# Reciprocals on a folded 96x6 tile, one key-sum addition open to two engines, weights converted by alternate eights, and PSUM banks dealt anew after batch 0

## Chip, cores and metric

The kernel runs on one core of one Trainium2 chip. The metric is the device time of one execution in microseconds (us). Five instruction streams matter: TensorE (PE in the profile, with its weight loads as PEld), VectorE (DVE), ScalarE (ACT), GpSimd (POOL) and SyncE (SP), which issues all the DMAs.

## What is computed

An attention over pooled queries feeds a two-layer network without a bias. Cut to what matters:

```python
q_pool = q.reshape(B, H, S // 2, 2, D).mean(axis=3)       # B, H, S, D = 4, 8, 1152, 64
scores = q_pool @ k^T / sqrt(D);  scores -= max(scores)    # 576 x 1152 for each head
attn   = exp(scores) / (sum(exp(scores)) + 1e-9)
x      = (attn @ v) of all heads side by side              # 2304 x 512
h      = x @ w_in;  g = maximum(0.01 * h, h);  out = g @ w_out   # d_ff = 2048
```

All inputs are float32 except for the weights, which arrive as float64 and are converted on the chip.

## The kernel before

**Stages.** There are 32 heads (4 batches of 8). For each head `k_tr`, `q_sum` and `q_tr` bring keys and queries into transposed form, each split in a high and a low part; `qk` (15 matmuls) with `vmax` (a DVE maximum of each result) and `vneg` find the row maxima, which `m_cp` and `m_dma` write into the query tile. A head has two units `u` of 288 queries. For each unit five groups `qkt` (four matmuls, the last group two) write scores into a PSUM slot `s`, `exp` on ACT empties the slot into one of seven tiles `e`, `esum` adds the five tiles up in five additions (four of them over the tiles, the last folding the two halves), and `pv` multiplies with the values. `norm` collects the two halves of `pv`. When both units are done, `r_mm` (L424) sums over the keys' partitions, `r_cp` (ACT) copies the sums to the tile `rs`, `r_inv` (L442) takes their reciprocals on all 128 x 288 elements, `scale` (POOL) multiplies and `x_out` writes the head's part of x to DRAM.

The second part works on 9 blocks of 256 rows of x. `l1` (L552: 16 chunks `f` of w_in with 12 matmuls of 256 columns each) fills PSUM tiles `ml`, `post` (ACT, then DVE or ACT, then POOL) makes the high and low parts `gg`, and `l2` (L574 to L576: three matmuls of 512 columns for each `f`) accumulates eight `f` in another `ml` tile, twice for each half of the rows. Block 0 needs batch 0 of x, so no `l1` can run before head 7's `x_out`.

**Weights.** Each of the 16 chunks of w_in and of w_out goes through `w_load` (DMA), `w_f32` in five steps (L484 ACT, L489 and L493 DVE, L497 ACT, L500 POOL), `w_hi` (a cast on DVE or ACT) and `w_lo` (L509 POOL); for w_in `w_out_dma` writes the result to DRAM, and `ws_load` fetches it for every block. All 16 chunks of w_in are converted first, then the 16 of w_out.

**What sets the order.** A planner in the kernel (`Scheduler`) takes steps by priority and by its own costs and writes one fixed instruction order for each engine. A step names the engines that may do it, and the planner takes the one that would be done first. PSUM has eight banks, dealt by name: `s` has two slots of two banks (0 and 1, 2 and 3), `t` (transposes, `qk`, `r_mm`) banks 4 and 7, with bank 6 until batch 0 is done, `o` (`pv`) bank 5, and `ml` bank 6 from then on; behind the last `pv` `ml` has six more.

```python
tags["s"] = [(None, 0, slots("bank", (0, 1), (2, 3)))]
tags["ml"] = [(early, 0, slots("bank", (6,))), (tail, 0, slots("bank", (0,), (1,), (2,), (3,), (4,), (7,)))]
step(esum, u, NX, prio=pu - 3, eng={"POOL": gp(HW)}, deps=[("esum", u, NX - 1)])
step(r_inv, hd, prio=pu - 2, eng={"DVE": 0.15 + 8 * HW / 960.0}, deps=... [("r_cp", hd)])
```

Of the kernel before, what the change touches and what calls it, by code (L numbers as in the profile page):

```python
# [149 lines left out]
def tile_pooled_attention_moe(  # L150
# [246 lines left out]
    def by_pe(hd):  # L397
        return hd < PESUM

    def over_keys(p, u, w):  # L400
        for x in range(NX):
            ts = kts(x)
            for a in range(2):
                if len(ts) == 2:
                    t, c = ts[a], slice(0, HW)
                    s = ex[u, x][:, a]
# [7 lines left out]
    def pv(u, e, i, i2=None):
        po[u] = new("o", i)
        over_keys(po[u], u, lambda t: vv[u // 2][:, t, :])
        if i2 is not None:
            rps[u] = new("t", i2)
            over_keys(rps[u], u, lambda t: ones)
# [361 lines left out]
```

## Time and profile before

| what | us |
|---|---|
| median of 3 runs | 1021.51 |
| the runs | 1017.75 to 1022.74 |
| the profiled execution | 1023.68 |
| its span, first to last instruction | 1021.9 |
| PE busy in the span | 934.3 |
| POOL, DVE, ACT busy | 634.0, 568.3, 426.4 |
| mean granted TensorE clock | 0.968 of full |

A busy time is a sum over the instructions of an engine, waits for a shared port inside an instruction among it. The granted clock is the share of full speed that TensorE was given: 1.0 is 2.4 GHz and 0.5 is 1.2 GHz. Heads are told apart in the trace by `r_mm`, which stands once in each.

### The profile page before, as it was taken

How to read it: one execution, taken by the hardware profiler on the slowest of the kernel's cores; microseconds unless marked ns; L12 is line 12 of the kernel's file. 1: busy time of each engine (PE TensorE's matmuls, PEld its weight loads, DVE VectorE, ACT ScalarE, POOL GpSimd, SP SyncE). 2: the span in 40 equal slices, each digit the busy share in tenths (PEclk: the TensorE clock that was granted, in tenths of full speed). 3: DMA queues.
4: the chain of work that ended last, by engine and by line, in shares of the span. 5: the costliest groups of instructions: out<-in, count | busy, mean ns of one | idle time of the engine just before them, and what ended most of it. 6: DMA issues, size and time to landing. Idle time of an engine off the chain costs nothing.

```text
span 1021.9 us, 16164 instructions
## 1 busy us (share of the span) xinstructions
PE 934.3 (91%) x5920; PEld 741.2 (73%) x5920; DVE 568.3 (56%) x934; ACT 426.4 (42%) x856; POOL 634.0 (62%) x548
## 2 busy tenths in 40 slices
PE   6888886978978898999999999999999999999998
PEld 2665654647845687777777778787788898989896
DVE  5799888787778888766666666666211111010100
ACT  3565654545655556555445545544221111111110
POOL 3688888578978889867657767748832222232320
PEclk9998988989978999999999999999999999999999
DMA  9264444365514236435415345214386565666640
GB/s 262 88 200 156 151 128 126 106 214 187 208 58 151 85 116 191 133 86 163 135 53 173 110 122 174 85 51 141 95 260 211 195 207 184 201 207 208 212 154 31
DMA packets 96943, 153.72 MB, mean 150 GB/s; under 512 B 9408, under 2 KB 63840, under 8 KB 96864
## 3 DMA queue, kind: packets, MB, share of 16 engines
q1 hardware_dynamic: 96864, 152.68, 47.8%
q8 instruction: 47, 0.77, 0.3%
q14 instruction: 32, 0.26, 0.1%
HBM read 125.30 MB, written 17.83 MB: 140 GB/s over the span
## 4 chain that ended last, share of the span: by engine, by line
PE 71%; DVE 10%; issue 5%; ACT 5%; POOL 4%; DMA 3%; SPq 2%; DVEq 0%; ACTq 0%; POOLq 0%
PE banks L552 19%; PE banks L410 12%; PE banks L347 9%; PE banks L378 6%; PE banks L379 6%; PE banks L574 5%; PE banks L575 5%; PE banks L576 5%; DVE stat L351 3%; DMA xb<-xd 2%; SPq L530 2%; DVE raw L493 1%; PE banks L424 1%; DVE raw L489 1%; ACT qh L325 1%
## 5 line engine op out<-in xcount | busy, mean ns | idle before, releaser
L351 DVE TENSOR_REDUCE stat<-banks 128x1 f32<-128x384 f32 (+1 forms) x480 | 255.0, 550 | 106.5 <-PE banks L347 94.2
L552 PE MATMUL banks<-xb,ws 128*128 128x256 f32 x1728 | 238.5, 285 | 9.4 <-issue 3.1
L552 PEld LDWEIGHTS banks<-xb,ws 128*128 128x128 f32 x1728 | 225.6, 191 | 20.4 <-issue 5.7
L384 ACT ACTIVATE e<-banks 128x576 f32<-128x576 f32 (+1 forms) x320 | 183.9, 600 | 128.8 <-PE banks L379 62.6
L392 POOL TENSOR_TENSOR sm<-sm,e 128x576 f32<-128x576 f32 (+1 forms) x192 | 234.9, 1242 | 0.5
L347 PE MATMUL banks<-ka,qh 128*128 128x384 f32 (+1 forms) x480 | 176.7, 399 | 38.2 <-DVE ql L329 20.0
L378 PE MATMUL banks<-qh,ka 128*128 128x288 f32 x576 | 172.9, 316 | 12.9 <-ACT e L384 12.0
L379 PE MATMUL banks<-ql,kb 128*128 128x288 f32 x576 | 165.1, 302 | 0.3 <-DMA ql<-ms 0.3
L410 PE MATMUL banks<-e,vv 128*64 128x288 f32 (+1 forms) x1280 | 164.5, 406 | 0.4 <-ACT e L384 0.4
L347 PEld LDWEIGHTS banks<-ka,qh 128*128 128x128 f32 (+1 forms) x480 | 86.8, 190 | 77.3 <-DVE stat L351 30.3
L410 PEld LDWEIGHTS banks<-e,vv 128*64 128x64 f32 x1280 | 90.3, 144 | 71.9 <-issue 23.0
L565 POOL TENSOR_TENSOR gg<-g,gg 128x512 fp32r<-128x512 f32 x50 | 64.9, 1298 | 116.3 <-DVE gg L191 106.6
L378 PEld LDWEIGHTS banks<-qh,ka 128*128 128x128 f32 x576 | 112.4, 195 | 28.5 <-ACT e L384 23.1
L560 ACT ACTIVATE g<-banks 128x512 f32<-128x512 f32 x72 | 43.1, 598 | 214.2 <-PE banks L552 214.0
L392 POOL TENSOR_TENSOR sm<-e 128x576 f32<-128x576 f32 x64 | 91.8, 1451 | 58.5 <-PE banks L424 53.2
L379 PEld LDWEIGHTS banks<-ql,kb 128*128 128x128 f32 x576 | 112.5, 195 | 1.3 <-DMA ql<-ms 0.5
L574 PE MATMUL banks<-wo,gg 128*128 128x512 f32 x200 | 81.1, 406 | 0.6 <-ACT raw L191 0.3
L191 DVE CAST gg<-g 128x512 fp32r<-128x512 f32 x40 | 21.8, 546 | 106.0 <-ACT g L560 106.0
L565 POOL TENSOR_TENSOR ka<-g,ka 128x512 fp32r<-128x512 f32 x22 | 28.3, 1288 | 81.3 <-DVE ka L191 70.7
L575 PE MATMUL banks<-wo,gg 128*128 128x512 f32 x200 | 78.5, 393 | 0.0
L576 PE MATMUL banks<-wo,gg 128*128 128x512 f32 x200 | 78.3, 392 | 0.0
L442 DVE RECIPROCAL rs<-rs 128x288 f32<-128x288 f32 x32 | 62.4, 1949 | 12.3 <-ACT rs L428 12.0
(61 smaller groups left out, 1066.4 us busy)
## 6 DMA issues: line engine op xcount, KB each, us to landing
ws<-wd SPq DMA_DIRECT2D x144, 512.0 KB
kn<-in_k_dram SPq DMA_DIRECT2D x32, 288.0 KB
qn<-in_q_dram SPq DMA_DIRECT2D x32, 288.0 KB
vv<-in_v_dram SPq DMA_DIRECT2D x32, 288.0 KB
raw<-in_moe_w_in_dram SPq DMA_DIRECT2D x16, 512.0 KB
kb<-ka SPq DMA_DIRECT2D x64, 128.0 KB
wd<-ws SPq DMA_DIRECT2D x16, 512.0 KB
raw<-in_moe_w_out_dram SPq DMA_DIRECT2D x16, 512.0 KB
```

The source lines that it names most:

```text
L347: nc.tensor.matmul(p, lhsT=qh[hd][:, o:o + n], rhs=ka[hd][:, c * CW:(c + 1) * CW], start=True, stop=True)
L351: nc.vector.tensor_reduce(out=mx[hd][:n, i, c:c + 1], in_=mps.pop((hd, i, c)), axis=AX.X, op=ALU.max)
L378: nc.tensor.matmul(p[:, a, :HW], lhsT=ka[hd][:, ks], rhs=qh[hd][:, c], start=True, stop=False)
L379: nc.tensor.matmul(p[:, a, :HW], lhsT=kb[hd][:, ks], rhs=ql[hd][:, c], start=False, stop=True)
L384: nc.scalar.activation(out=ex[u, x][:, :n], in_=sps.pop((u, x))[:, :n, :HW], func=AF.Exp)
L392: ENG[e].tensor_tensor(out=a, in0=ex[u, 0][:, :n] if x == 1 else a, in1=ex[u, x][:, :n], op=ALU.add)
L410: nc.tensor.matmul(p[64 * a:64 * a + 64, c], lhsT=w(t), rhs=s, start=(x == 0), stop=(x == NX - 1))
L552: nc.tensor.matmul(p, lhsT=wst[i, f][:, a, c, :], rhs=xx[i][:, x, c, :], start=(n == 0), stop=(n == 3 * KC - 1))
L565: ENG[e].tensor_tensor(out=t[:, 1], in0=gf.pop((i, fp)), in1=f32(t[:, 0]), op=ALU.subtract)
L574: nc.tensor.matmul(p, lhsT=gh, rhs=wo[f][:, 0], start=(f == hf * FH), stop=False)
L575: nc.tensor.matmul(p, lhsT=gh, rhs=wo[f][:, 1], start=False, stop=False)
L576: nc.tensor.matmul(p, lhsT=gl, rhs=wo[f][:, 0], start=False, stop=(f == hf * FH + FH - 1))
```

## The change

- **Reciprocals.** `r_cp` is followed by `r_fold` (two small DMAs that fold one row of each half of `rs` into a tile `rt` of 96 x 6), `r_inv` on `rt`, `r_row` (a DMA of `rt` to DRAM) and `r_wide` (two DMAs that spread it over the 128 partitions of `rs` again). `rs` has two buffers in place of one.
- **Key sums.** The addition `x == 2` of each unit may go to DVE, at the planner's cost plus 0.4; the fixed order puts 54 of the 64 there.
- **Weights.** The order is eight chunks of w_in, eight of w_out, eight of w_in, eight of w_out; `w_hi` is on ACT alone; `w_load` may run four ahead instead of three, and the priorities change.
- **PSUM.** When batch 0 is done, `s` keeps one slot (0 and 1), `t` gets bank 2 and `ml` bank 3 beside bank 6.
- The branch `by_pe`, which `PESUM = 0` had switched off, is gone.

```diff
-PESUM = 0
+DX = (2,)
+CONT = 0.4
-WAHEAD = 3
-WIN = (30.0, 0.5)
+WAHEAD = 4
+WIN = (40.0, 0.5)
...
-        "rs": (1, [128, HW], F32, sb),
+        "rs": (2, [128, HW], F32, sb),
+        "rt": (2, [SP // RN, RN], F32, sb),
...
-    tags["s"] = [(None, 0, slots("bank", (0, 1), (2, 3)))]
-    tags["t"] = [(None, 0, slots("bank", (4,), (7,))), (None, early, slots("bank", (6,)))]
+    tags["s"] = [(None, 0, slots("bank", (0, 1))), (None, early, slots("bank", (2, 3)))]
+    tags["t"] = [(None, 0, slots("bank", (4,), (7,))), (None, early, slots("bank", (6,))), (early, 0, slots("bank", (2,)))]
...
-    tags["ml"] = [(early, 0, slots("bank", (6,))), (tail, 0, slots("bank", (0,), (1,), (2,), (3,), (4,), (7,)))]
+    tags["ml"] = [(early, 0, slots("bank", (6,), (3,))), (tail, 0, slots("bank", (0,), (1,), (2,), (3,), (4,), (7,)))]
...
+    def r_fold(hd, e, i):
+        rts[hd] = new("rt", i)
+        for hf in range(2):
+            src = rss[hd][64 * hf:64 * hf + 1].rearrange("o (a n) -> o a n", n=RN)
+            nc.sync.dma_start(out=rts[hd][HW // RN * hf:HW // RN * (hf + 1)], in_=src)
 
     def r_inv(hd, e):
-        nc.vector.reciprocal(out=rss[hd], in_=rss[hd])
+        nc.vector.reciprocal(out=rts[hd], in_=rts[hd])
+
+    def r_row(hd, e):
+        nc.sync.dma_start(out=rd[hd].rearrange("h (a n) -> (h a) n", n=RN), in_=rts.pop(hd))
+
+    def r_wide(hd, e):
+        for hf in range(2):
+            nc.sync.dma_start(out=rss[hd][64 * hf:64 * hf + 64], in_=rd[hd][hf:hf + 1].to_broadcast([64, HW]))
...
+    def adds(n, x):
+        return {"POOL": gp(n), "DVE": dve(n) + CONT} if x in DX else {"POOL": gp(n)}
...
+    seq = [o * NF + g * FH + i for g in range(2) for o in range(2) for i in range(FH)]
+    for n, i in enumerate(seq):
...
-        step(w_hi, i, prio=pr, eng={"ACT": act(512), "DVE": dve(512, 2)}, deps=[("w_f32", i, 4)], takes=[] if o else [("ws", [("w_out_dma", i)])])
+        step(w_hi, i, prio=pr, eng={"ACT": act(512)}, deps=[("w_f32", i, 4)], takes=[] if o else [("ws", [("w_out_dma", i)])])
```

The planner writes a new order for every engine. On DVE, the order of before around the reciprocal of head 5 (`ql` is the low part of the queries of a later head, `x` is `norm`):

```order
L489 TENSOR_SCALAR raw<-raw 128x512
L493 SCALAR_TENSOR_TENSOR raw<-raw 128x512
L453 TENSOR_TENSOR x_1507<-banks,t_1506 64x288
L329 SCALAR_TENSOR_TENSOR ql_72<-banks,qh 64x3x96
L442 RECIPROCAL rs<-rs 128x288
L191 CAST ws<-raw 128x512
L329 SCALAR_TENSOR_TENSOR ql_72<-banks,qh 64x3x96
L292 TENSOR_TENSOR ka<-banks,ka 64x4x128
```

The same place in the changed kernel (lines are those of the changed file; L396 is `esum`):

```order
L485 TENSOR_SCALAR raw<-raw 128x512
L358 TENSOR_REDUCE neg_69<-stat_66 128x5
L333 SCALAR_TENSOR_TENSOR ql_72<-banks,qh 64x3x96
L489 SCALAR_TENSOR_TENSOR raw<-raw 128x512
L396 TENSOR_TENSOR sm<-sm,e 128x576 x2
L333 SCALAR_TENSOR_TENSOR ql_72<-banks,qh 64x3x96
L431 RECIPROCAL rt<-rt 96x6
L296 TENSOR_TENSOR ka<-banks,ka 64x4x128 x2
```

The cast has left DVE, two additions have come, and the reciprocal is on the small tile.

On PE, the order of before in the first unit of head 20, from the second `qkt` group to the fourth:

```order
L378 MATMUL banks<-qh,ka 128x288
L379 MATMUL banks<-ql_72,kb_70 128x288
L378 MATMUL banks<-qh,ka 128x288
L379 MATMUL banks<-ql_72,kb_70 128x288
L378 MATMUL banks<-qh,ka 128x288
L379 MATMUL banks<-ql_72,kb_70 128x288
L378 MATMUL banks<-qh,ka 128x288
L379 MATMUL banks<-ql_72,kb_70 128x288
L347 MATMUL banks<-ka,qh 128x384
L318 MATMUL banks<-ident,qs 128x96 x3
```

The same groups in the changed kernel (L382 and L383 are `qkt`, L351 `qk`, L570 to L572 `l2`):

```order
L382 MATMUL banks<-qh,ka 128x288
L383 MATMUL banks<-ql_72,kb_70 128x288
L382 MATMUL banks<-qh,ka 128x288
L383 MATMUL banks<-ql_72,kb_70 128x288
L351 MATMUL banks<-ka,qh 128x384 x2
L570 MATMUL banks<-wo,gg 128x512
L571 MATMUL banks<-wo,gg 128x512
L572 MATMUL banks<-wo,gg 128x512
L382 MATMUL banks<-qh,ka 128x288
L383 MATMUL banks<-ql_72,kb_70 128x288
L382 MATMUL banks<-qh,ka 128x288
L383 MATMUL banks<-ql_72,kb_70 128x288
```

Two groups that stood one behind the other now have other work between them. How much of the second part stands ahead of a head's `r_mm` in the two orders, in matmuls (of 1728 `l1` and 864 `l2`):

| ahead of the `r_mm` of head | 7 | 8 | 9 | 11 | 13 | 15 | 31 |
|---|---|---|---|---|---|---|---|
| before: `l1`, `l2` | 0, 0 | 16, 0 | 60, 0 | 96, 0 | 96, 27 | 184, 48 | 656, 264 |
| after: `l1`, `l2` | 0, 0 | 0, 0 | 40, 0 | 120, 30 | 208, 51 | 240, 81 | 732, 324 |

## Rows read from the trace of the kernel before

**Rows 1.** The page: granted TensorE clock in 40 slices, in tenths.

```profile
PEclk9998988989978999999999999999999999999999
```

**Rows 2.** Timeline of PE: r_mm of heads 0, 7, 15, 31 (start, length).

```profile
62.27 0.71 PE L424 MATMUL banks<-sm,ones 128*64 128x288 f32 x4
...
210.53 0.71 PE L424 MATMUL banks<-sm,ones 128*64 128x288 f32 x4
...
403.98 0.71 PE L424 MATMUL banks<-sm,ones 128*64 128x288 f32 x4
...
741.91 0.71 PE L424 MATMUL banks<-sm,ones 128*64 128x288 f32 x4
```

**Rows 3.** Stretches: length; PE, PEld, DVE, ACT, POOL busy; clock; DMA share; GB/s.

```profile
62.00:211.00 149.00, 123.99 (x739) 84.06 (x737) 129.09 (x197) 84.33 (x172) 119.53 (x105) 0.90 0.44 139
211.00:404.00 193.00, 166.93 (x1064) 126.59 (x1062) 155.06 (x243) 109.89 (x221) 168.20 (x140) 0.92 0.46 150
404.00:742.00 338.00, 327.98 (x2246) 260.02 (x2247) 210.12 (x362) 163.52 (x337) 241.03 (x213) 1.00 0.39 118
742.00:1022.00 280.00, 269.53 (x1676) 240.40 (x1676) 30.77 (x58) 38.72 (x65) 72.06 (x52) 1.00 0.59 187
```

**Rows 4.** Timeline of PE behind the last head: l1 and l2 in turn.

```profile
783.49 3.04 PE L552 MATMUL banks<-xb,ws 128*128 128x256 f32 x24
786.36 0.39 PE L574 MATMUL banks<-wo,ka 128*128 128x512 f32 x1
...
787.77 3.02 PE L552 MATMUL banks<-xb,ws 128*128 128x256 f32 x24
```

**Rows 5.** Groups on DVE, 62 to 211 us (count, busy, mean ns, idle before).

```profile
L191 DVE CAST ws<-raw 128x512 fp32r<-128x512 f32 x7 | 16.5, 2362 | 0.0
L493 DVE SCALAR_TENSOR_TENSOR raw<-raw 128x512 uint32<-128x512 uint32 x11 | 14.2, 1290 | 0.3
L442 DVE RECIPROCAL rs<-rs 128x288 f32<-128x288 f32 x7 | 13.6, 1949 | 1.2 <-ACT rs L428 1.1
```

**Rows 6.** Groups on DVE, 211 to 404 us.

```profile
L442 DVE RECIPROCAL rs<-rs 128x288 f32<-128x288 f32 x8 | 15.6, 1944 | 0.1
...
L191 DVE CAST wo<-raw 128x512 fp32r<-128x512 f32 x8 | 10.8, 1352 | 0.1
```

**Rows 7.** Timelines of DVE, POOL and PE around a cast at 165 us.

```profile
165.21 9.52 DVE L191 CAST ws<-raw 128x512 fp32r<-128x512 f32 x1
...
165.99 1.41 POOL L392 TENSOR_TENSOR sm<-sm,e 128x576 f32<-128x576 f32 x1
...
174.81 1.27 POOL L509 TENSOR_TENSOR ws<-raw,ws 128x512 fp32r<-128x512 f32 x1 [0.37 <-DVE ws L191]
...
175.28 0.69 PE L347 MATMUL banks<-ka,qh 128*128 128x384 f32 x1 [8.37 <-DVE ql L329]
```

**Rows 8.** Timeline of DVE: step L493 while POOL was idle.

```profile
101.27 0.69 DVE L493 SCALAR_TENSOR_TENSOR raw<-raw 128x512 uint32<-128x512 uint32 x1
```

**Rows 9.** Waits for exp in 404 to 742 us (total, times, longest); one exp.

```profile
PE banks L378 <- ACT e L384: 2.9, 4, 1.7
...
PEld banks L378 <- ACT e L384: 5.5, 9, 2.1
...
163.76 0.65 ACT L384 ACTIVATE e<-banks 128x576 f32<-128x576 f32 x1
```

**Rows 10.** Small DMA, its user; a wait for a larger one.

```profile
192.83 0.75 SPq L365 DMA_DIRECT2D ql<-ms  x1
...
194.66 0.40 PE L379 MATMUL banks<-ql,kb 128*128 128x288 f32 x1 [0.33 <-DMA ql<-ms]
...
954.41 0.70 DVE L191 CAST xb<-xb 128x1024 fp32r<-128x1024 f32 x1 [3.78 <-DMA xb<-xd]
```

**Rows 11.** Small and narrow DVE and POOL groups of the whole span.

```profile
L354 DVE TENSOR_REDUCE neg<-stat 128x5 f32<-128x15 f32 x32 | 5.2, 161 | 0.6
...
L565 POOL TENSOR_TENSOR gg<-g,gg 128x512 fp32r<-128x512 f32 x50 | 64.9, 1298 | 116.3 <-DVE gg L191 106.6 <-issue 6.4 <-ACT gg L191 3.2
```

More of the change, by code (lines that the diff above doesn't have):

```diff
@@ L244, in tile_pooled_attention_moe @@
     xd = [dram.tile([DM, SP], F32, name=f"xd{b}") for b in range(B)]
+    rd = [dram.tile([2, HW], F32, name=f"rd{j}") for j in range(NHD)]
     wd = [dram.tile([128, 2, KC, 128], F32, name=f"wd{f}") for f in range(NF)]
@@ L404, in over_keys @@
                 if len(ts) == 2:
[L405 to L406 removed]
+                    t, c, s = ts[a], slice(0, HW), ex[u, x][:, a]
                 else:
@@ L410, in over_keys @@
                 nc.tensor.matmul(
-                    p[64 * a:64 * a + 64, c], lhsT=w(t), rhs=s, start=(x == 0), stop=(x == NX - 1)
+                    p[64 * a:64 * a + 64, c], lhsT=vv[u // 2][:, t, :], rhs=s, start=(x == 0), stop=(x == NX - 1)
                 )
[L414 to L419, printed above, removed]
     def r_mm(hd, e, i):
@@ L668, in tile_pooled_attention_moe @@
                 step(exp, u, x, prio=pu - 5, eng={"ACT": act(n * HW, True)}, deps=[("qkt", u, x)],
-                     takes=[("e", [("pv", u)] + ([] if by_pe(hd) else [("esum", u, max(x, 1))]))])
-                if x and not by_pe(hd):
-                    step(esum, u, x, prio=pu - 4 + 0.2 * x, eng={"POOL": gp(n * HW)}, deps=[("exp", u, x), ("exp", u, 0) if x == 1 else ("esum", u, x - 1)],
+                     takes=[("e", [("pv", u), ("esum", u, max(x, 1))])])
+                if x:
+                    step(esum, u, x, prio=pu - 4 + 0.2 * x, eng=adds(n * HW, x), deps=[("exp", u, x), ("exp", u, 0) if x == 1 else ("esum", u, x - 1)],
                          takes=[("sm", [("r_mm", hd)])] if x == 1 else [])
-            if not by_pe(hd):
-                step(esum, u, NX, prio=pu - 3, eng={"POOL": gp(HW)}, deps=[("esum", u, NX - 1)])
+            step(esum, u, NX, prio=pu - 3, eng=adds(HW, NX), deps=[("esum", u, NX - 1)])
             cols = [HW] * (NX - 1) + [HW // 2]
-            step(pv, u, prio=pu + PVP, eng=mm4(*cols * (2 if by_pe(hd) else 1)), deps=[("exp", u, x) for x in range(NX)] + [("load_v", hd), ("pv", u - 1) if u else None],
-                 takes=[("o", [("norm", u, 1)])] + ([("t", [("r_half", u, 1)])] if by_pe(hd) else []))
+            step(pv, u, prio=pu + PVP, eng=mm4(*cols), deps=[("exp", u, x) for x in range(NX)] + [("load_v", hd), ("pv", u - 1) if u else None],
+                 takes=[("o", [("norm", u, 1)])])
             step(norm, u, 0, prio=pu - 2, eng={"ACT": act(HW, True)}, deps=[("pv", u)],
@@ L680, in tile_pooled_attention_moe @@
             step(norm, u, 1, prio=pu - 2, eng={"DVE": dve(HW, psum=True)}, deps=[("norm", u, 0)])
-            if by_pe(hd):
-                step(r_half, u, 0, prio=pu - 2, eng={"ACT": act(HW, True)}, deps=[("pv", u)],
-                     takes=[("t1", [("r_half", u, 1)])] + ([("rs", [("scale", hd)])] if hf == 0 else []))
-                step(r_half, u, 1, prio=pu - 2, eng={"DVE": dve(HW, psum=True)}, deps=[("r_half", u, 0)])
-            elif hf:
+            if hf:
                 step(r_mm, hd, prio=pu + RT, eng=mm4(HW), deps=[("esum", u - 1, NX), ("esum", u, NX)], takes=[("t", [("r_cp", hd)])])
@@ L687, in tile_pooled_attention_moe @@
                 step(r_cp, hd, prio=pu - 2, eng={"ACT": act(HW, True)}, deps=[("r_mm", hd)], takes=[("rs", [("scale", hd)])])
-            if hf:
-                step(r_inv, hd, prio=pu - 2, eng={"DVE": 0.15 + 8 * HW / 960.0}, deps=[("r_half", u, 1), ("r_half", u - 1, 1)] if by_pe(hd) else [("r_cp", hd)])
-                step(scale, hd, prio=pu - 2, eng={"POOL": gp(HW)}, deps=[("r_inv", hd), ("norm", u, 1), ("norm", u - 1, 1)])
+                step(r_fold, hd, prio=pu - 2, **sp(2, 0.002e6), deps=[("r_cp", hd)], takes=[("rt", [("r_row", hd)])])
@@ L691, in tile_pooled_attention_moe @@
+                step(r_inv, hd, prio=pu - 2, eng={"DVE": 0.2}, deps=[("r_fold", hd)])
+                step(r_row, hd, prio=pu - 2, **sp(1, 0.002e6), deps=[("r_inv", hd)])
+                step(r_wide, hd, prio=pu - 2, **sp(2, 0.15e6), deps=[("r_row", hd)])
+                step(scale, hd, prio=pu - 2, eng={"POOL": gp(HW)}, deps=[("r_wide", hd), ("norm", u, 1), ("norm", u - 1, 1)])
                 step(x_out, hd, prio=pu - 2, **sp(2, 0.15e6), deps=[("scale", hd)])
-    for i in range(2 * NF):
+    seq = [o * NF + g * FH + i for g in range(2) for o in range(2) for i in range(FH)]
```

27 lines of the change are left out of this document (9 added, 18 removed).

## The prediction

> **What bounds the kernel now.** I read the page's clock line, then the timeline of PE for `r_mm`, which stands once in each head, and cut the span there into stages. The clock line falls below 0.9 only in slices 4 to 13 of 40, between 77 and 332 us [rows 1]. `r_mm` of heads 0, 7, 15 and 31 stands at 62, 211, 404 and 742 us [rows 2]. The busy times of these stretches [rows 3] tell three regimes. From 404 us on PE is busy for 328 of 338 us and 270 of 280 us at clock 1.00: PE is the limit. From 62 to 211 us PE is busy for 124 of 149 us at a mean clock of 0.90, while DVE is busy 129 us (0.866 of the stretch) and POOL 120. From 211 to 404 us the clock is 0.92, POOL is busy 168 of 193 us (0.871) and DVE 155. There PE waits for the other two.
>
> How much PE time is lost follows from the work. In the long run behind the last head, 24 matmuls of `l1` take 786.36 - 783.49 = 2.87 us, 0.120 each, and six of `l2` take 787.77 - 786.36 = 1.41 us, 0.235 each [rows 4]. From head 15 to 31 stand 472 `l1` and 216 `l2` (the counts in the table of the change), 56.6 + 50.8 = 107.4 us of the 328; the rest is 220.6 us, 13.8 for each of 16 heads. So stage 62 to 211 holds 7 x 13.8 = 97 us of PE work and loses 52; stage 211 to 404 holds 8 x 13.8 + 184 x 0.120 + 48 x 0.235 = 144 us and loses 49. The two stages lose 101 us together, and only this can be won in quantity. Before 62 us nothing of the change bears; I leave that at 62.
>
> **Part 1, reciprocals.** In 62 to 211 us seven of 1.949 us are taken off DVE, 13.6 us [rows 5], in the next stage eight, 15.6 us [rows 6]. A reciprocal on 6 columns is not in the trace; between nothing and the nearest small DVE instruction, 0.161 us [rows 11], I take the latter: 1.1 us for seven, 1.3 for eight. In their place come five DMAs for each head on SP. The small `ql` DMA was issued at 192.83 and PE could go on at 194.66, 1.8 us [rows 10]. Three legs in a row, with a second issue of about 0.75 us in two of them, make some 7 us from `r_cp` to `scale`, 5 more than now. Only `scale` and `x_out` hang on them, and they are hurried once, at head 7: the order puts the first `l1` behind head 8's `r_mm`, where 16 stood ahead of it (table of the change). DVE now waits for a DMA in front of `r_inv`, with `vmax` queued behind it; on SP `r_row` and `r_wide` hold up whatever load stands next. A late leg would cost its lateness in each head, but the one planned small DMA that the trace has made PE wait 0.33 us once [rows 10]; I take nothing, and up to 0.3 x 15 = 5 us for the range.
>
> **Part 2, casts and weights' order.** All `w_hi` casts leave DVE. Alone such a cast would be short, but seven took 16.5 us [rows 5], eight more 10.8 us [rows 6]. One ran 9.52 us, from 165.21 to 174.73: it ended when POOL had its first gap, of 0.37 us, and PE, waiting for the `ql` queued behind it, stood for 8.37 us [rows 7]. That is gone. ACT takes the casts; it is busy 84 of 149 and 110 of 193 us [rows 3], which covers them. The alternate order lets `l2` begin ahead of head 11's `r_mm`, where it began behind it, so that `l1`, which stood at 96 from head 11 to head 13, no longer stops; I price that within stage two's sum.
>
> **Part 3, additions.** 54 of 64 `x == 2` additions go to DVE, two for a head. On POOL one takes 1.41 us [rows 7]. On DVE it is not in the trace. L493 also has two SBUF inputs, of 512 columns: 0.69 us when POOL was idle [rows 8], so 0.78 for 576; the other end is the mean cast, 2.36 us [rows 5]. I take 1.3 us, nearest to L493's mean of 1.29 beside a busy POOL [rows 5]. POOL in turn may be held up by half of 0.78, so I count a relief of 1.0.
>
> What POOL loses is not all gained, by the Trainium skill ("SBUF — State Buffer", section "Who interferes with whom"): a VectorE instruction with two SBUF inputs and a GpSimd instruction that reads SBUF block each other for their whole length. L493's 0.69 against 1.29 us agrees; what full blocking gives is rival A.
>
> **The sum of the stages.** *62 to 211:* DVE 129.1 - 13.6 + 1.1 - 16.5 + 14 x 1.3 = 118.3 us; at the share of now, 0.866, 137 us. POOL falls by 14, so DVE stays the limit. *211 to 404:* POOL 168.2 - 16 x 1.0 = 152.2; by head 15 56 more `l1` have been done, some three more `post` of 1.3 us [rows 11], so 156.1; at 0.871, 179 us. DVE, 155.1 - 15.6 + 1.3 - 10.8 + 16 x 1.3 = 150.8, is below it, and PE's work, 110 + 240 x 0.120 + 81 x 0.235 = 158, too. *404 to 742:* 732 - 240 = 492 `l1` and 324 - 81 = 243 `l2`, 20 and 27 more than now: 2.4 + 6.3 = 8.7 us, so 347. *Behind head 31:* 76 `l1` and 60 `l2` fewer: 9.1 + 14.1 = 23.2 us, so 257.
>
> **Part 4, PSUM.** After batch 0 the next `qkt` group waits for the `exp` of the last: 0.65 us [rows 9] and a hand-over on either side, which I put at 0.1 each, 0.85 together. With two slots PE and its weight loads waited 2.9 and 5.5 us in 160 groups [rows 9]. Counting the other PE work between two groups in the new order by the costs above (and `pv` and transposes by the same stretch), 212 of 230 groups from head 9 on have over 0.85 us; 18 fall short, by 6.5 us together. I take 5. The third bank for `t` and the second for `ml` I cost at nothing beyond the moved `l1` and `l2` that they allow.
>
> The span becomes 62 + 137 + 179 + 347 + 257 + 5 = 987 us. The profiled execution took 1023.7 us, 1.8 more than its span and 2.2 more than the median. So 987 + 1.8 = 989 against 1023.7, and **987 us** against the median of 1021.5; the rivals' sums take the same 1.8 - 2.2 = -0.4.
>
> **Rivals.**
> *A, full blocking.* Each moved addition keeps POOL out for its whole 0.78 us, so the relief is 0.63, and costs DVE 1.5 (half a POOL instruction of 1.41 ahead of it). Stage one 100.1 + 21 = 121.1 over 0.866 = 140, stage two 168.2 - 10.1 + 3.9 = 162 over 0.871 = 186: 62 + 140 + 186 + 347 + 257 + 5 - 0.4 = 997 us. L493's long cases speak for it; that it has no waits like the cast's speaks for less.
> *B, the early stages nearly reach PE.* With the stalls like that at 165 us gone, stage two runs at PE's pace, 158 us of work at the share of 328 in 338, 163 us; stage one with additions of 0.78 us is 111 over 0.866 = 128; the single slot costs nothing: 62 + 128 + 163 + 347 + 257 - 0.4 = 957 us. The casts' share of the waits speaks for it; POOL's load in stage two speaks against.
> *C, the additions starve like the casts.* At 2.36 us each, stage one is 133.1 over 0.866 = 154, stage two, now DVE's, 167.8 over 0.87 = 193: 62 + 154 + 193 + 347 + 257 + 5 - 0.4 = 1018 us, no change. L493, in the same place before, speaks against.
> *D, slower: the single slot.* ACT works in order, and if an `exp` comes late behind another instruction PE stands, since nothing overtakes a `qkt`. At 0.25 us for each of 230 groups this is 57 in place of 5: 1039 us. It decides from (1023.7 - 984) / 230 = 0.17 us a group. ACT is busy for 164 of 338 us [rows 3], so half of the `exp` could find it occupied; the filler in the order speaks against. The same time comes out where DVE waits 1.8 us for the fold in every early head and passes it on to PE.
> That the additions stay on POOL is excluded by the order.
>
> **Chances and range.** Forecast 0.57, A 0.18, B 0.12, C 0.06, D 0.07. The range leaves out C, D and half of B, 0.19: 957 to 1012 us, which takes in A with the 5 us of late legs and more. Half a per cent, 5 us, is about what a measurement of this kernel can tell from no change: faster by more 0.87 (the forecast, A and B), the same 0.06 (C), slower 0.07 (D).
>
> **What would show it.** Right: `r_mm` of head 7 near 199 us, of head 15 near 378, of head 31 near 725; clock at full from an earlier slice; the addition on DVE near 1.3 us; `l1` without a stop; PE waits for `exp` below 10 us behind batch 0. Wrong: `r_mm` of head 15 later than 395 (A or C, told apart by the addition's mean on DVE), 404 to 742 grown by over 20 us with waits of `qkt` for `exp` (D), or DVE idle in front of the small reciprocal for a DMA. The forecast fails most easily at the shares: if DVE's and POOL's busy times fall but the stretches don't, another wait was the limit there.

## The result and the profile after

The changed kernel takes 993.2 us (median; 990.5 to 995.1) against 1020.6 (1017.8 to 1022.7) beside it: a ratio of 0.9735, 95% interval 0.9715 to 0.9754. That is faster, 6 us above the forecast of 987 and inside its range. The profiled execution took 995.1 us, its span 993.3.

The page of the changed kernel: busy times of the engines, and the granted clock in 40 slices.

```profile
PE 919.2 (93%) x5920; PEld 735.6 (74%) x5920; DVE 538.6 (54%) x973; ACT 440.0 (44%) x871; POOL 571.7 (58%) x494
...
PEclk9999889989999999999989999999999999999999
```

The timeline of PE at `r_mm` (L418 now) of heads 0, 7, 15 and 31, which answers to [rows 2]:

```profile
56.23 0.71 PE L418 MATMUL banks<-sm,ones 128*64 128x288 f32 x4
...
203.46 0.71 PE L418 MATMUL banks<-sm,ones 128*64 128x288 f32 x4
...
391.61 0.71 PE L418 MATMUL banks<-sm,ones 128*64 128x288 f32 x4
...
740.03 0.71 PE L418 MATMUL banks<-sm,ones 128*64 128x288 f32 x4
```

The stretches between these marks (columns as in [rows 3]):

```profile
0.00:56.20 56.20, 42.35 (x198) 27.75 (x198) 40.00 (x76) 27.61 (x55) 28.41 (x37) 1.00 0.69 206
56.20:203.50 147.30, 123.78 (x742) 84.40 (x741) 124.57 (x208) 94.98 (x192) 116.17 (x100) 0.92 0.50 147
203.50:391.60 188.10, 169.17 (x1114) 132.28 (x1113) 150.68 (x249) 111.52 (x226) 155.69 (x127) 0.96 0.57 178
391.60:740.00 348.40, 340.84 (x2331) 274.61 (x2330) 195.23 (x385) 170.75 (x342) 204.65 (x184) 0.99 0.43 125
740.00:993.30 253.30, 243.10 (x1541) 216.54 (x1540) 28.14 (x56) 35.10 (x59) 66.81 (x48) 1.00 0.59 191
```

The same stretches of before, cut at its own marks:

```profile
0.00:62.30 62.30, 46.18 (x207) 30.29 (x207) 43.55 (x79) 30.27 (x62) 33.46 (x41) 0.97 0.64 190
62.30:210.50 148.20, 123.19 (x733) 83.70 (x732) 128.29 (x196) 83.94 (x172) 119.08 (x104) 0.90 0.44 139
210.50:404.00 193.50, 167.43 (x1067) 126.82 (x1066) 155.56 (x244) 109.98 (x222) 168.34 (x140) 0.92 0.46 149
```

The last two stages of before were 337.9 and 280.0 us. So the five stages moved by -6.1, -0.9, -5.4, +10.5 and -26.7 us, together -28.6. Seen from PE, the span is its busy time and its gaps: gaps fell from 1021.9 - 934.3 = 87.6 to 993.3 - 919.2 = 74.1 us, and the same matmuls took 15.1 us less, with the mean clock up from 0.968 to 0.976. So half of the gain is shorter gaps, and the other half shorter matmuls. The mean clocks account for about 934.3 x (1 - 0.968 / 0.976) = 7.7 of those 15.1 us (an estimate); where the rest comes from is open.

### The profile page after: what moved, and what is told of

It is laid out like the page before. It is cut to its first block, busy times and chain, and to the rows that moved or that the text cites. A ratio compares the mean times of both kernels' runs of the same rounds, so it can differ in the third digit from the quotient of the medians.

```text
span 993.3 us, 16418 instructions
## 1 busy us (share of the span) xinstructions
PE 919.2 (93%) x5920; PEld 735.6 (74%) x5920; DVE 538.6 (54%) x973; ACT 440.0 (44%) x871; POOL 571.7 (58%) x494
## 4 chain that ended last, share of the span: by engine, by line
PE 66%; DVE 11%; DMA 9%; POOL 5%; ACT 4%; issue 4%; SPq 2%; DVEq 0%; POOLq 0%; ACTq 0%
PE banks L548 17%; PE banks L411 11%; PE banks L351 7%; PE banks L382 7%; PE banks L383 5%; PE banks L570 5%; PE banks L571 5%; PE banks L572 5%; DVE stat L355 3%; DMA xb<-xd 2%; DMA rd<-rt 2%; DVE raw L485 2%; DVE sm L396 1%; PE banks L418 1%; DMA rt<-rs 1%
## 5 line engine op out<-in xcount | busy, mean ns | idle before, releaser
L355 DVE TENSOR_REDUCE stat<-banks 128x1 f32<-128x384 f32 (+1 forms) x480 | 245.9, 549 | 37.1 <-PE banks L351 30.4
L388 ACT ACTIVATE e<-banks 128x576 f32<-128x576 f32 (+1 forms) x320 | 190.7, 602 | 142.9 <-PE banks L383 131.8
L396 POOL TENSOR_TENSOR sm<-sm,e 128x576 f32<-128x576 f32 (+1 forms) x138 | 161.3, 1175 | 56.9 <-ACT e L388 30.6
L382 PE MATMUL banks<-qh,ka 128*128 128x288 f32 x576 | 179.1, 325 | 10.1 <-ACT e L388 9.8
L351 PE MATMUL banks<-ka,qh 128*128 128x384 f32 (+1 forms) x480 | 154.6, 378 | 23.3 <-DVE ql L333 11.9
L383 PE MATMUL banks<-ql,kb 128*128 128x288 f32 x576 | 164.8, 300 | 0.7 <-DMA ql<-ms 0.7
L382 PEld LDWEIGHTS banks<-qh,ka 128*128 128x128 f32 x576 | 111.2, 193 | 36.6 <-ACT e L388 22.8
L396 POOL TENSOR_TENSOR sm<-e 128x576 f32<-128x576 f32 x64 | 92.8, 1454 | 75.1 <-ACT e L388 64.1
L561 POOL TENSOR_TENSOR gg<-g,gg 128x512 fp32r<-128x512 f32 x52 | 68.5, 1317 | 89.8 <-DVE gg L193 71.3
L351 PEld LDWEIGHTS banks<-ka,qh 128*128 128x128 f32 (+1 forms) x480 | 82.4, 185 | 50.5 <-DVE stat L355 19.8
L383 PEld LDWEIGHTS banks<-ql,kb 128*128 128x128 f32 x576 | 111.5, 194 | 2.6 <-issue 0.9
L570 PE MATMUL banks<-wo,gg 128*128 128x512 f32 x208 | 82.9, 398 | 0.0
L571 PE MATMUL banks<-wo,gg 128*128 128x512 f32 x208 | 82.2, 395 | 0.0
L572 PE MATMUL banks<-wo,gg 128*128 128x512 f32 x208 | 82.0, 394 | 0.0
L396 DVE TENSOR_TENSOR sm<-sm,e 128x576 f32<-128x576 f32 x54 | 59.7, 1109 | 21.0 <-ACT e L388 12.1
L193 ACT COPY t<-banks 64x288 f32<-64x288 f32 x64 | 25.2, 394 | 98.7 <-PE banks L411 98.4
```

Source lines behind the costliest of these rows:

```text
L351: nc.tensor.matmul(p, lhsT=qh[hd][:, o:o + n], rhs=ka[hd][:, c * CW:(c + 1) * CW], start=True, stop=True)
L355: nc.vector.tensor_reduce(out=mx[hd][:n, i, c:c + 1], in_=mps.pop((hd, i, c)), axis=AX.X, op=ALU.max)
L382: nc.tensor.matmul(p[:, a, :HW], lhsT=ka[hd][:, ks], rhs=qh[hd][:, c], start=True, stop=False)
L383: nc.tensor.matmul(p[:, a, :HW], lhsT=kb[hd][:, ks], rhs=ql[hd][:, c], start=False, stop=True)
L388: nc.scalar.activation(out=ex[u, x][:, :n], in_=sps.pop((u, x))[:, :n, :HW], func=AF.Exp)
L396: ENG[e].tensor_tensor(out=a, in0=ex[u, 0][:, :n] if x == 1 else a, in1=ex[u, x][:, :n], op=ALU.add)
```

## Experiments

All the medians, and the stages of each profiled execution (us; kernels above the line are the changed one with something undone or altered, below it the one before with something done). Each kernel is one order of the planner, and the order also settles how many of the `x == 2` additions go to DVE: 54 in the changed kernel, 39 in u_recip, 38 in o_psum_add, 55 to 60 in the others that let them go there and none in u_add, o_psum and before. One stage in one execution is no exact figure either: up to head 7 u_psum has the changed kernel's order on every engine, and yet that stage took 150.7 us for 147.3.

| kernel | median | to head 0 | to 7 | to 15 | to 31 | tail |
|---|---|---|---|---|---|---|
| before | 1020.6 | 62.3 | 148.2 | 193.5 | 337.9 | 280.0 |
| changed | 993.2 | 56.2 | 147.3 | 188.1 | 348.4 | 253.3 |
| u_add | 1006.4 | 56.1 | 137.3 | 213.0 | 328.9 | 270.6 |
| u_psum | 1015.4 | 56.0 | 150.7 | 196.5 | 332.4 | 278.2 |
| u_recip | 990.1 | 56.5 | 149.2 | 189.1 | 340.2 | 254.6 |
| u_weights | 985.7 | 61.1 | 136.5 | 178.4 | 342.3 | 263.7 |
| u_weights_nocast | 997.7 | 60.3 | 144.8 | 184.3 | 340.0 | 264.6 |
| u_cast | 1010.6 | 55.9 | 141.4 | 197.6 | 347.7 | 259.9 |
| w_seq | 987.9 | 56.5 | 144.5 | 183.9 | 342.7 | 259.6 |
| conv_light | 985.5 | 55.2 | 148.8 | 180.5 | 344.1 | 252.8 |
| more_dve | 1029.0 | 56.6 | 152.2 | 195.9 | 362.6 | 252.0 |
| reorder | 985.7 | 53.5 | 143.4 | 188.9 | 337.3 | 259.8 |
| — | | | | | | |
| o_psum | 1019.0 | 61.5 | 147.5 | 195.6 | 334.3 | 277.4 |
| o_psum_add | 1000.7 | 63.6 | 148.7 | 185.7 | 340.6 | 263.0 |

### Each part undone

*u_add*, all additions on POOL again:

```diff
-DX = (2,)
+DX = ()
```

> The changed kernel with all key-sum additions on POOL again (DX empty), the other parts kept. In its order 652 l1 and 285 l2 stand ahead of head 31's r_mm, 80 and 39 fewer than in the changed kernel, so the stretch behind it should grow by 80 x 0.120 + 39 x 0.235 = 19 us. Theory (POOL's load is what keeps the second part out of the attention): 1010 to 1015 us, with head 31's r_mm within 8 us of 740. Rival (a moved addition blocks POOL through the shared port for as long as it relieves it): 990 to 998 us, with head 31's r_mm earlier by what the tail gains.

*u_psum*, the old banks:

```diff
-    tags["s"] = [(None, 0, slots("bank", (0, 1))), (None, early, slots("bank", (2, 3)))]
+    tags["s"] = [(None, 0, slots("bank", (0, 1), (2, 3)))]
...
-    tags["ml"] = [(early, 0, slots("bank", (6,), (3,))), (tail, 0, slots("bank", (0,), (1,), (2,), (3,), (4,), (7,)))]
+    tags["ml"] = [(early, 0, slots("bank", (6,))), (tail, 0, slots("bank", (0,), (1,), (2,), (3,), (4,), (7,)))]
```

> The changed kernel with the PSUM banks dealt as before: two slots for the scores, one bank for the second part during the attention. 632 l1 and 264 l2 ahead of head 31's r_mm: the tail grows by 100 x 0.120 + 60 x 0.235 = 26 us; between heads 15 and 31 the work falls by 76 x 0.120 + 60 x 0.235 = 23 us. Theory (the second bank only moves work from a stage where PE is the limit anyway): that stage shrinks by as much and the time stays at 990 to 1000 us. Rival (without the bank PE idles, the stage keeps its length): 1010 to 1020 us. Second rival (the single slot of the changed kernel costs 0.1 us or more a group): faster than 985 us.

*u_recip*, the old reciprocal with one `rs` buffer and none of the five DMAs:

```diff
-        nc.vector.reciprocal(out=rts[hd], in_=rts[hd])
+        nc.vector.reciprocal(out=rss[hd], in_=rss[hd])
```

> The changed kernel with the reciprocal on all 128 x 288 elements again and without the five DMAs for each head. Its order has the same 732 l1 and 324 l2 ahead of head 31's r_mm; 39 additions are on DVE in place of 54. Theory (DVE is the limit up to head 7 alone, and PE behind it hides the rest): 7 x 1.8 = 12 us more on DVE up to head 7, so 997 to 1005 us. Rival (the 62 us of reciprocals were the whole gain): 1015 us or more. Third case (the DMA chain costs as much as the reciprocals gave): 988 to 995 us.

*u_weights*, the old treatment of the weights (order, priorities, loads ahead, casts, costs):

```diff
-WAHEAD = 4
-WIN = (40.0, 0.5)
+WAHEAD = 3
+WIN = (30.0, 0.5)
...
-        step(w_f32, i, 2, prio=pr, eng={"DVE": dve(512) + CONT}, deps=[("w_f32", i, 1)])
+        step(w_f32, i, 2, prio=pr, eng={"DVE": dve(512)}, deps=[("w_f32", i, 1)])
```

> The changed kernel with all of w_in converted ahead of w_out again, w_hi open to DVE (12 casts go there), the old priorities and no extra cost for DVE's weight steps. 708 l1 and 291 l2 ahead of head 31's r_mm, so the tail grows by 24 x 0.120 + 33 x 0.235 = 11 us. Theory (starved casts and a late first l2 cost time between heads 3 and 13): 1005 to 1012 us with casts of several us. Rival (order of conversion is indifferent, since the same conversions stand in the same busy stretch): 990 to 998 us.

Measured: without the additions 1006.4 (1005.3 to 1007.9; ratio to before 0.987), without the banks 1015.4 (1012.4 to 1023.2; 0.997), with the old reciprocal 990.1 (987.5 to 991.5; 0.971), with the old weights 985.7 (983.8 to 988.8; 0.968). Undoing the banks thus costs the changed kernel 22 us and undoing the additions 13; undoing the reciprocal costs nothing, and undoing the weights' part seems to gain 7. u_psum lies in its first rival's range and u_recip in its third case's; u_add lies between its two ranges, and u_weights below both of its own. u_weights also has the highest granted clock of all: 0.984 to 0.988 in its four runs, where the changed kernel has 0.974 to 0.978. At some 920 us of PE work 0.010 of the clock is 9 us (an estimate), as much as it gains.

What the banks do themselves is seen best behind head 15. The last two stretches of u_psum, and its waits of PE in the first of them (total us, times, longest):

```profile
403.20:735.60 332.40, 317.75 (x2156) 248.35 (x2155) 220.07 (x390) 158.87 (x328) 198.73 (x176) 0.99 0.40 116
735.60:1013.80 278.20, 268.70 (x1701) 238.68 (x1700) 30.21 (x60) 38.68 (x65) 73.43 (x54) 1.00 0.59 193
```

```profile
PE banks L351 <- DVE stat L355: 6.9, 10, 1.9
```

PE stands for 332.4 - 317.8 = 14.7 us there, 7.6 in the changed kernel: `qk` (L351) waits for `vmax` to empty one of only two `t` banks. Its order has 100 `l1` and 60 `l2` more behind head 31, 100 x 0.120 + 60 x 0.235 = 26.1 us by [rows 4], and the tail is 24.9 us longer, while the stage before it is 16.0 shorter, so the rival was right in the time and only in part in its reason. Together that is 8.9 us of the 20.5 by which its profiled execution is longer. Another 8.4 stand between heads 7 and 15, where no run tells the banks from the order, and 3.4 up to head 7, where the order is the same and the banks are not yet dealt anew: those are scatter.

### The banks alone, and with the additions

*o_psum* takes the banks of the change into the kernel before and nothing else, *o_psum_add* the banks and

```diff
-                    step(esum, u, x, prio=pu - 4 + 0.2 * x, eng={"POOL": gp(n * HW)}, deps=...
+                    step(esum, u, x, prio=pu - 4 + 0.2 * x, eng=adds(n * HW, x), deps=...
```

> The kernel before with the PSUM banks dealt as in the change, and nothing else. Theory (parts add up: undone from the changed kernel the banks cost 22 us): 995 to 1001 us. Rival (the banks let l1 and l2 come earlier only as far as POOL and DVE deliver, and POOL still has all the additions; with the additions back on POOL the changed kernel took 1006): 1004 to 1012 us, with the last stage still near 268.

> The kernel before with the PSUM banks dealt as in the change and the two additions of a head open to DVE; reciprocals, weights' order and casts as before. Theory: these two parts carry the whole gain, the folded reciprocal gives nothing and the new treatment of the weights costs some 7 us. Undone singly from the changed kernel, the reciprocal left 990 us and the weights 986, so without both 980 to 990 us. Rival: each of the two only looked idle because the other covered for it (the reciprocal on 128 x 288 and the casts both stand on DVE beside the additions, 13.6 + 16.5 us in the first stage); with both back on DVE the first two stages grow by 10 to 20 us: 995 to 1005.

Measured: the banks alone 1019.0 (1015.5 to 1022.4; 0.9999, interval 0.998 to 1.002), slower than either expectation; with the additions 1000.7 (999.4 to 1003.5; 0.981, interval 0.979 to 0.983), in the rival's range. But the rival's reason did not come true: it wanted the two stages up to head 15 longer by 10 to 20 us, and they took 148.7 + 185.7 = 334.4, where the changed kernel took 335.4. The start (63.6) and the tail (263.0) are longer. POOL in 209 to 405 us of o_psum suggests why the banks do nothing alone (group: count, busy us, mean ns, idle before):

```profile
L392 POOL TENSOR_TENSOR sm<-sm,e 128x576 f32<-128x576 f32 (+1 forms) x48 | 61.8, 1291 | 0.2
```

POOL is never idle ahead of these additions, and 180 `l1` are done when head 15 is, 184 without the banks: more room for `l1` is no use while POOL is late with the sums. This is not the whole reason, since POOL is as late between heads 7 and 15 of u_add (193.4 to 406.4 us):

```profile
L396 POOL TENSOR_TENSOR sm<-sm,e 128x576 f32<-128x576 f32 (+1 forms) x48 | 60.4, 1268 | 0.0
```

and u_add, with the banks, the folded reciprocal and the weights' part but without the additions, is 12 us faster than before. So the parts are not independent: the banks are worth nothing alone, 1001 with just the additions beside them, 1006 with all but the additions; and all but the banks is 1015, 3 us better than before. Which of the other parts lets the banks pay in u_add was not tried.

### Is DVE's or POOL's load the limit of the early stages?

*conv_light* cuts two of a weight chunk's steps from 512 columns to 16, in an unchanged order (a part of the conversion is left out), *more_dve* adds two reciprocals on a scratch tile in each head:

```diff
-                out=wt[i], in0=w[:, :, 0], scalar=29, in1=wt[i], op0=ALU.logical_shift_right, op1=ALU.bitwise_or
+                out=wt[i][:, :16], in0=w[:, :16, 0], scalar=29, in1=wt[i][:, :16], op0=ALU.logical_shift_right, op1=ALU.bitwise_or
...
-            nc.gpsimd.tensor_tensor(out=wt[i], in0=wt[i], in1=wy[i], op=ALU.mult)
+            nc.gpsimd.tensor_tensor(out=wt[i][:, :16], in0=wt[i][:, :16], in1=wy[i][:, :16], op=ALU.mult)
```

```diff
+        nc.vector.reciprocal(out=pad, in_=pad)
+        nc.vector.reciprocal(out=pad, in_=pad)
```

> The changed kernel in its own instruction order, with two steps of each weight chunk cut from 512 columns to 16: the shift and or on DVE (L489) and the multiplication on POOL (L496). So a part of the weights' conversion is left out, and the work of DVE and POOL falls by some 1 us and 1.3 us for each of 13 chunks up to head 7's r_mm and of 15 up to head 15's. Theory of the prediction (the share at which DVE or POOL is busy is the limit): the stage up to head 7 shortens by 13 x 1.2 = 15 us or more, the stage to head 15 by 15 to 20 us, span some 960. Rival (PE waits there for chains of hand-overs in a fixed order, and the load of one engine is not the limit): each of the two stages shortens by 5 us at most, span 985 to 993.

> The changed kernel in its own instruction order with two more reciprocals of 128 x 128 on a scratch tile on DVE in each head, in front of the head's small reciprocal: some 1.8 us more DVE work a head, 13 us up to head 7 and 14 us from there to head 15. Theory (DVE's busy share is the limit): the stage up to head 7 grows by 13 / 0.85 = 15 us, the whole by 15 to 30. Rival (hand-overs are the limit, DVE has room between): each of the two stages grows by 4 us at most and the whole time by less than 8 us.

conv_light took 985.5 us (983.2 to 987.5). Its stretch up to head 7, and the waits of PE in it:

```profile
55.20:204.00 148.80, 124.98 (x741) 84.98 (x739) 115.64 (x208) 95.56 (x194) 97.58 (x99) 0.91 0.49 145
```

```profile
PE banks L382 <- ACT e L388: 6.0, 10, 1.4
PE banks L351 <- DVE ql L333: 5.0, 4, 2.9
PE banks L351 <- DVE ka L296: 2.1, 2, 1.4
```

The changed kernel in the same stage:

```profile
PE banks L382 <- ACT e L388: 6.0, 9, 1.5
PE banks L351 <- DVE ql L333: 5.3, 3, 2.9
PE banks L351 <- DVE ka L296: 2.1, 2, 1.4
```

DVE is relieved of 8.9 us and POOL of 18.6, the stage is no shorter (+1.5, within the scatter), and PE waits at the same lines for about the same times. Up to head 7 the load that the conversions put on these two engines is not the limit. The second stage became 7.6 us shorter, so there it may be in part: more than the rival's 5, less than the theory's 15. The third, which holds no conversion at all, became 4.3 shorter too, and that is the granted clock:

```profile
384.50:728.60 344.10, 336.49 (x2331) 271.99 (x2330) 195.49 (x385) 171.13 (x342) 205.07 (x184) 1.00 0.44 127
```

PE's gaps are 7.6 us in both kernels, and its busy time is 4.35 us less at clock 1.00 in place of 0.99.

A stage with much less DVE work can be shorter, though: u_add's two stretches up to head 15, in another order, are

```profile
56.10:193.40 137.30, 120.87 (x730) 81.82 (x729) 95.19 (x183) 81.35 (x167) 110.66 (x98) 0.93 0.46 137
193.40:406.40 213.00, 178.01 (x1101) 133.02 (x1100) 150.62 (x257) 127.32 (x251) 185.90 (x153) 0.94 0.55 168
```

Up to head 7 DVE has 29.4 us less to do than in the changed kernel and the stage is 10.0 us shorter. More conversions stand behind head 7 in that order (22 multiplications on POOL for 15), and the second stage is 24.9 us longer.

more_dve took 1029.0 us; its profiled execution, 1021.2, is the fastest of eight, the others lie at 1028 to 1031, so its stages show somewhat less than the usual cost. The added pair takes 0.91 + 0.95 = 1.86 us: 13.0, 14.9 and 29.8 us in the three stages up to head 31, which grew by 4.9, 7.8 and 14.2. That is 0.4 to 0.5 us for each us (0.6 by the medians, 35.8 us for 59.5), in the third stage as in the first, though DVE had been busy there for 0.56 of the time and in the first for 0.85. Its third stage, and what PE waited for in it (0.8 us in the changed kernel):

```profile
404.70:767.30 362.60, 341.53 (x2331) 273.24 (x2330) 221.91 (x417) 170.84 (x342) 204.35 (x184) 1.00 0.42 120
```

```profile
PE banks L352 <- DVE stat L356: 17.5, 12, 3.1
```

A late `vmax` leaves `qk` without a bank. Neither expectation held. DVE's share of busy time tells neither of the two results; where in the chain of hand-overs the microsecond stands seems to decide, which no run tested by itself.

### Which piece of the weights' part?

*u_weights_nocast* is u_weights with `w_hi` on ACT alone; *u_cast* is the changed kernel with

```diff
-        step(w_hi, i, prio=pr, eng={"ACT": act(512)}, deps=...
+        step(w_hi, i, prio=pr, eng={"ACT": act(512), "DVE": dve(512, 2)}, deps=...
```

and *w_seq* the changed kernel with the chunks in the old order:

```diff
-    seq = [o * NF + g * FH + i for g in range(2) for o in range(2) for i in range(FH)]
+    seq = list(range(2 * NF))
```

> The changed kernel with the weights in the old order, priorities, costs and three loads ahead, but w_hi on ACT alone. It splits the 7 us which the weights' part costs. If the casts on ACT are what costs (ACT's exp come later), this stays at 991 to 995 us. If the order, the priorities and the dearer DVE costs are what costs, this comes to 984 to 988 us, as with all of the part undone.

> The changed kernel, but w_hi may go to ACT or DVE as before (15 of the 32 casts then stand on DVE in the fixed order); the alternate order of the chunks, the priorities, the dearer DVE costs and four loads ahead stay. With the weights' part undone as a whole the kernel took 985.7 us, and with all of it undone but the casts 997.7, so in the old order the casts on ACT cost 12 us. Theory (the casts' move is what costs; the new priorities keep their start, 56 us in place of 61): 978 to 985 us, with stages one and two near 137 and 178. Rival (what the casts do hangs on the order around them, and in the new order they cost nothing): 990 to 996 us.

> The changed kernel with the chunks in the old order, 16 of w_in and then 16 of w_out; casts on ACT alone, dearer DVE costs and the rest of the change stay. If the alternate order gains what the prediction gave it (l2 begins two heads earlier, l1 does not stop), this takes 996 to 1003 us with a longer second stage. If it gains nothing, 991 to 995 us.

Measured: 997.7 (996.2 to 998.6), 1010.6 (1004.7 to 1011.9, the profile is of the fastest) and 987.9 (986.7 to 989.0). The first and the second lie above both of their ranges. In the old order casts on DVE save 12 us, in the new one they cost 17, so these runs give the casts no price of their own. The alternate order has not gained anything either: w_seq lies below both expectations, 5 us faster than the kernel with it.

### Order alone

*reorder* moves one number of the planner that the change leaves as it was, and nothing in the steps:

```diff
-LAT = 0.12
+LAT = 0.125
```

> The changed kernel with one number of the planner moved that the change does not touch: the hand-over it plans between two engines, 0.125 us in place of 0.12. The same instructions come out in another order on every engine (59 additions on DVE in place of 54; 236 l1 and 78 l2 ahead of head 15's r_mm, 696 and 318 ahead of head 31's). It measures how much of the differences between single edits is order alone. Theory (the edits' effects do not add up because each edit draws a new order, and an order by itself is worth some 5 to 15 us): this lies 5 us or more from the changed kernel's 993.2, on either side, and the stages move against one another by as much as in the edits that were undone. Rival (orders of the same work are worth 3 us at most, and the interactions between the parts are real): 990 to 996 us.

Measured: 985.7 us (981.7 to 986.8; ratio to before 0.965, interval 0.962 to 0.969), 7.5 below the changed kernel with no run in common, in the theory's range. The granted clock is not the reason: 0.972 to 0.979 here, 0.974 to 0.978 there. Its stretches:

```profile
0.00:53.50 53.50, 40.54 (x200) 28.02 (x200) 39.35 (x77) 27.62 (x55) 27.29 (x36) 1.00 0.73 218
53.50:196.90 143.40, 122.35 (x742) 84.79 (x741) 123.24 (x210) 95.60 (x193) 116.34 (x100) 0.92 0.51 154
196.90:385.80 188.90, 169.88 (x1104) 129.75 (x1103) 152.10 (x247) 110.44 (x223) 152.60 (x126) 0.95 0.55 173
385.80:723.10 337.30, 331.61 (x2301) 267.41 (x2302) 198.76 (x392) 168.53 (x339) 198.64 (x180) 1.00 0.44 127
723.10:982.90 259.80, 249.71 (x1586) 222.26 (x1582) 28.24 (x56) 36.74 (x62) 68.17 (x49) 1.00 0.58 190
```

The loads in the early stages are the changed kernel's within 1 to 3 us. So a new order of the same steps, with five more additions on DVE in it, is worth 7.5 us here, and the 3 us of the reciprocal, the 7.5 of the weights' part and the 5 of the chunks' order can't be told from it. One such draw doesn't say how far orders scatter. What stands above it is the group: the eight kernels that have both the banks and the additions open to DVE (conv_light and more_dve aside) take 986 to 1011 us, the three that lack one 1006 to 1019 and the kernel before, which lacks both, 1021; only u_cast and u_add overlap. The 25 us from end to end of the first group are a warning for the 13 of the additions and the 22 of the banks, each of which rests on one order. reorder and u_weights beat both the changed kernel and the one before.

## Why the prediction was right, and where it was not

*What bounds the kernel.* "There PE waits for the other two" is true of the waits, but the size was off: 13.8 us of PE work a head came from the stage behind head 15. In the first stage 733 / 7 = 105 matmuls stand for each head, where the late stage has (2244 - 688) / 16 = 97. PE's busy time by the clock gives 123.2 x 0.90 = 111 us before and 123.8 x 0.92 = 114 after, so this stage lost 37 us and not 52. The next lost 193.5 - 167.4 x 0.92 = 39 and not 49.

*Start.* I left it at 62 us; it is 56.2. In part that is the mark, since 198 matmuls in place of 207 stand ahead of it, so it is better read with the next stage: `r_mm` of head 7 came 7.0 us earlier, forecast 12.

*The stages up to head 15: the step that failed* is "at the share of now". The terms under it came close: in the second stage POOL 155.7 us (156.1 forecast) and DVE 150.7 (150.8). But the stage didn't follow: 188.1 for 179, and the first 147.3 for 137. In the first, DVE fell to 124.6 only (118.3 forecast), because I held the conversions fixed. The order put 14 of the steps L489 there (L493 before, 11 in [rows 5]) and 13 of the `TENSOR_SCALAR` steps ahead of them (L485, below in part 3), where 11 stood before; each of the latter also took longer, 1.12 us for 0.79:

```profile
L489 DVE TENSOR_SCALAR raw<-raw 128x512 uint32<-128x512 uint32 x11 | 8.7, 789 | 0.6 <-ACT raw L484 0.4
```

POOL lost only 2.9 us there of the 14 forecast, since the order gave it 29 conversion steps in place of 20. That is the smaller matter: conv_light took the load away, and the stage stayed. Nor is the share a ceiling. u_weights has the same DVE load up to head 7, 125.7 us, in 136.5 us, a share of 0.921, with PE's gaps at 20.4 us and the clock at 0.96:

```profile
61.10:197.60 136.50, 116.13 (x730) 79.72 (x730) 125.75 (x216) 91.13 (x184) 117.07 (x97) 0.96 0.59 178
```

The 8.37 us stall behind the cast [rows 7] is gone as forecast, and PE's gaps still fell by just 25.0 - 23.5 = 1.5 us: other hand-overs took its place. PE waited 5.3 us for `ql` after 11.0, but 2.1 for `ka` after none and 6.0 for `exp` after 4.4, and many shorter waits make up the rest. By head 15 the kernel had won 12.4 us of the 26 forecast, and 6.1 of these before head 0, where none was forecast.

By the Trainium skill ("Perfetto Trace Analysis", section "Identifying the Most-Contended Engine") one finds the engine with the highest occupancy and optimizes it first, and so did I; that a stage shrinks in step with that engine's load was my own addition. In the first stage conv_light bears out neither: DVE's 0.846 became 0.777 for nothing.

*Part 1.* The reciprocal now takes 0.18 us, as assumed, and the removal of 1.95 us a head shows in no time (u_recip, whose order also gives 15 additions back to POOL). For head 15 the fold took 403.64 - 393.24 = 10.4 us from `r_cp` to `scale`, where I said 7, and POOL, the busiest engine of that stage beside PE, stood for it:

```profile
403.64 0.81 POOL L452 TENSOR_TENSOR x<-x,rs 128x288 f32<-128x288 f32 x1 [4.57 <-DMA rs<-rd]
```

I had priced such a wait on DVE, not on POOL, where it came to 8.0 us up to head 7 and 29.8 from head 15 to 31. That it cost the kernel time no run shows.

*Part 2.* Its gain was priced within the two stages and is not there; whether it costs is open, since u_weights' 7.5 us go with its clock and are no more than reorder's.

*Part 3.* DVE's groups up to head 7 and from there to head 15:

```profile
L396 DVE TENSOR_TENSOR sm<-sm,e 128x576 f32<-128x576 f32 x14 | 19.4, 1399 | 2.9 <-POOL sm L396 2.1 <-ACT e L388 0.7
L489 DVE SCALAR_TENSOR_TENSOR raw<-raw 128x512 uint32<-128x512 uint32 x14 | 14.8, 1060 | 0.3
L485 DVE TENSOR_SCALAR raw<-raw 128x512 uint32<-128x512 uint32 x13 | 14.5, 1118 | 0.7 <-ACT raw L480 0.3 <-POOL raw L496 0.3
...
L431 DVE RECIPROCAL rt<-rt 96x6 f32<-96x6 f32 x7 | 1.2, 177 | 0.0
```

```profile
L489 DVE SCALAR_TENSOR_TENSOR raw<-raw 128x512 uint32<-128x512 uint32 x15 | 23.5, 1566 | 0.1
...
L396 DVE TENSOR_TENSOR sm<-sm,e 128x576 f32<-128x576 f32 x13 | 15.2, 1169 | 1.9 <-POOL sm L396 1.6
```

1.40 and 1.17 us an addition for the 1.3 forecast; over the whole span the median is 0.76, the price of one that meets no POOL instruction (27 of the 54), and the longest took 2.93. Only in the first stage is the mean near rival A's 1.5. A's marks, 202 and 388 us for heads 7 and 15, lie nearer to the 203.5 and 391.6 measured than mine, but for a reason that conv_light denies for the first of them: it is not the load that sets it. POOL's additions in the whole span, before and after:

```profile
L392 POOL TENSOR_TENSOR sm<-sm,e 128x576 f32<-128x576 f32 (+1 forms) x192 | 234.9, 1242 | 0.5
```

```profile
L396 POOL TENSOR_TENSOR sm<-sm,e 128x576 f32<-128x576 f32 (+1 forms) x138 | 161.3, 1175 | 56.9 <-ACT e L388 30.6 <-DVE sm L396 18.7 <-DVE stat L355 4.1
```

They fell by 73.6 us, 1.36 for each addition moved, where I took 1.0 and A 0.63. One takes 1.44 there on average before, so nearly all that POOL lost was gained. Before, POOL was idle for 0.5 us ahead of them; now it waits for `exp`, so the sums come earlier. That the 13 us of u_add are owed to this is likely, but not shown.

*Part 4 was right in its mechanism.* The order's counts gave +9 and -23 us for the last two stages, with 5 for the single slot; measured +10.5 and -26.7. Some of the +10.5 is the granted clock of that execution: conv_light has the same order there and took 344.1 us at clock 1.00, +6.2. The slot cost less than 5: the waits of `qkt` for `exp` from head 15 to 31 are

```profile
PEld banks L382 <- ACT e L388: 3.5, 12, 0.4
```

with none of PE itself, against 2.9 and 5.5 us with two slots [rows 9]. Rival D is dead, and so is C: no addition starved as the casts had. What I did not see is that the parts hang on one another (the banks alone gave nothing); the sum took each by itself.

So the total was right in part by luck, because misses cancelled: the two early stages came out 10 + 9 us longer than forecast, the start 6, the third stage with its slot 4 and the tail 4 us shorter. At 993 it lies between my 987 and A's 997, nearer to A's. Of the marks I named, `r_mm` of heads 7, 15 and 31 came 4, 14 and 15 us later than said; the clock line has 0.9 or more from slice 10 on but for slice 21 (from slice 14 on before), and behind batch 0 PE waited 3.8 us for `exp`, as said.

*Left open:* why the first stage takes 137 to 151 us in all these orders with 111 to 114 us of PE work (in the two multiplied out above; of the changed kernel's 147.3 us some 10 more are the lower clock and 23.5 are PE's gaps), and whether the weights' part costs anything. Neither was settled by a run. The additions, the reciprocal and the weights' part were not tried alone on the kernel before, and no kernel but the changed one was drawn in two orders.

## What to carry to other kernels

Where a planner deals a fixed order, draw one or two more orders from it before an edit is praised or blamed for a per cent or so, and look at the granted clock of both. Busy share says which engine to look at, not what a microsecond on it is worth; take a microsecond away and put one in, and see what the stage does. Ask of each part what must be there for it to pay: here the room in PSUM gave nothing alone, and 19 us with two additions a head open to DVE.

## What the runs showed of the hardware

- An addition of 128 x 576 with two SBUF inputs on DVE has a median of 0.76 us and a mean of 1.11; 27 of the 54 meet no POOL instruction and take 0.71 to 0.76 us, the others up to 2.93. POOL's own multiplication L496 grew a little beside it, from 1.30 to 1.33 us up to head 7, and its full-size additions of 128 x 576 over the whole span from 1.44 to 1.47.
- A small DMA of 1.1 KB from SBUF to SBUF lands 2.4 us after its issue, the one of 72 KB from DRAM after 3.4 (medians). The fold's three legs take 10.4 us in all, of which the reciprocal is 0.17: they are mostly waiting.
- A DVE instruction that is 1.86 us longer in every head costs 0.4 to 0.6 of that in the time, whether DVE is busy for 0.85 or for 0.56 of the stage (more_dve).
